# More filler matmuls in the opening of a fused cross-attention and ReGLU kernel

## The chip, the core and the metric

The kernel runs on one core of one Trainium2 chip. The metric is the time of one execution on the device, in microseconds (us). A core has a matrix engine (TensorE, "PE" in the profile, with its weight loads as "PEld"), a vector engine (DVE), a scalar engine (ACT), a general engine (POOL) and a queue engine (SP); each takes its own instructions in order and waits on semaphores for the others. Data comes and goes by DMA.

## The reference

Two stages, the first feeding the second. B = 8 batches, H = 8 heads, S = 512 tokens, Ns = 32 state rows and D = 64.

```python
scores = scale * x @ state^T                 # per batch and head
xread  = softmax(scores) @ state             # 512 rows per batch
sread  = softmax(scale * state @ x^T) @ x    # 32 rows per batch
t = concat([xread, sread]), heads side by side         # 4352 x 512
out = (relu(t @ w_gate) * (t @ w_val)) @ w_out         # 512 -> 1536 -> 512
```

The inputs are float32; the kernel multiplies in bfloat16 and adds in float32.

## The kernel before, in words

For the 512 token rows of a batch, attention output times `w_gate` is never formed in two steps. The kernel multiplies the state by the weights first (`U`, made by `c_unit` for 256 columns of both weights or by `u_unit` for 512 columns of one) and then multiplies the softmax weights by `U` (`gv`). Twelve column blocks `jf` of 128 give the gated product `h_sb`, and the last product with `w_out` (`o_half`) is built from seven half-sized products, for which POOL makes sums and differences (`h_sums`, `h_last`).

The order of the first three and a half batches is written out by hand. A text, `program`, is a list of steps such as `xT.0.1`; a table, `steps`, maps each name to a function, and a loop calls them in turn. A step emits its instructions at the end of the queues of the engines that it uses, so the list fixes the order on each engine, and only semaphores move one engine against another. The steps that matter here, for batch 0:

- `spin.n`: n matmuls of 512 columns on a zeroed tile `warm` (line 572), into a PSUM bank of their own (`warm_ps`) that nobody reads. These are the fillers.
- `stc`, `stT`, `sto`: cast the state of batches 0 and 1, transpose it on PE (line 149), copy it to SBUF (line 156).
- `xh`: cast `x` for two heads; `xT.0.j`: transpose it on PE (lines 182 and 184); `xo.0.j`: copy the transpose out on DVE or ACT (line 188).
- `sc.0.k`: scores on PE (line 199); `ex`: exponential on ACT (line 203); `nr`: sum and reciprocal on DVE (lines 209 and 211); `nx`: scaling on DVE (line 215).
- `aT.0.k`: transpose of the softmax weights on PE (line 231); `ao`: copy out on DVE (line 235).
- `c.k.i`: state times weight columns on PE (line 311), where k = 0 and 1 are the batch and i is the block of 256 columns; `co`: copy out on ACT or DVE (line 331).
- `ga` and `gb`: the first and second half of the product with `U` on PE (line 336); `re` and `mu`: ReLU on ACT (line 363) and product on DVE (line 367).

PE's small results rotate through six PSUM banks, so a step can also wait until the copy of an older result has freed a bank.

The weights come in twelve DMAs of 256 columns each (`w_dma`, line 134), issued by POOL in the order gate, value, gate, value and so on, with batch 1 of `x` after the first four. Block i of `c` needs the i-th gate and value pieces. After batch 3 the rest of the schedule comes from loops with slots.

Of the kernel before, what the change touches and what calls it, by code (L numbers as in the profile page):

```python
# [16 lines left out]
def kernel(  # L17
# [9 lines left out]
    nc = tc.nc  # L27
# [38 lines left out]
    warm = gpool.tile([128, 512], BF16, name="warm", tag="g_sb")  # L66
# [6 lines left out]
    stT = const.tile([128, B, NJ, 64], BF16, name="stT")  # L73
# [4 lines left out]
    xf, xb, xT, e_sn, a_sn, ANS, U, hsb, sr_sb = {}, {}, {}, {}, {}, {}, {}, {}, {}  # L78
    copy = {"act": nc.scalar.copy, "dve": nc.vector.tensor_copy, "pool": nc.gpsimd.tensor_copy}

    def bank(name, o=None):

        if o is None:
            return ps_r.tile([128, 512], FP32, name=name, tag="r")
        return ps_o.tile([128, 512], FP32, name=name, tag=f"o{o}")
# [73 lines left out]
    def x_conv(b, half, eng):  # L159
        if half == 0:  # L160
            xb_alloc(b)
            xb[b] = xb[b].rearrange("p (c h d) -> p c h d", c=NC, h=H)
        hs = slice(HK * half, HK * half + HK)
        copy[eng](out=xb[b][:, :, hs].rearrange("p c h d -> p h c d"), in_=xf[b][:, hs])
# [387 lines left out]
    ws = ((moe_w_gate, wg_sb), (moe_w_val, wv_sb))  # L552
# [15 lines left out]
    warm_ps = bank("warm_ps", "w")  # L568
# [4 lines left out]

    def x_cast(b, i, eng):
        x_conv(b, i, eng)

    steps = {"spin": spin, "stc": state_conv, "stT": state_T, "sto": state_out, "xT": x_T, "xo": x_out,
             "sc": att_sc, "ex": att_exp, "nr": att_sum, "nx": att_scale, "aT": att_T, "ao": att_out,  # L580
             "c": c_unit, "co": c_out, "u": u_unit, "uo": u_out, "ga": lambda b, jf: gv(b, jf, (0,)),
             "gb": lambda b, jf: gv(b, jf, (1,)), "re": relu, "mu": mult, "oh": o_half, "oc": o_c, "oa": o_a, "os": o_s,
             "hs": h_sums, "hl": h_last, "ws": w_sum, "xd": lambda b: x_dma(b, (nc.sync,)), "xg": lambda b: x_dma(b, (nc.gpsimd,)),
             "xh": x0_cast, "xc": x_cast,
             "xt": x_trans_dma, "aD": att_aT_dma, "srp": sr_pre, "srl": sr_low, "srm": sr_mm, "srn": sr_norm}
    program = """
    spin.7 stc.0.2.dve stT.0.2 sto.0.2.1.act sto.0.2.0.dve xh.0.dve xT.0.0 xo.0.0.dve xh.1.act xT.0.1
    xo.0.1.dve xT.0.3 xo.0.3.act sc.0.0 ex.0.0 xT.0.2 nr.0.0 nx.0.0 xo.0.2.act sc.0.1 ex.0.1 spin.1 c.0.0
    c.1.0 spin.1 nr.0.1 nx.0.1 aT.0.0 ao.0.0.dve spin.1 aT.0.1 co.0.0.0.act ga.0.0 co.1.0.0.act co.1.0.1.dve
    co.0.0.1.act ao.0.1.dve xg.3 c.0.1 co.0.1.0.act co.0.1.1.dve c.1.1 co.1.1.0.dve gb.0.0 re.0.0 mu.0.0  # L590
    ga.0.2 gb.0.2 re.0.2 mu.0.2 co.1.1.1.act ga.0.3 gb.0.3 re.0.3 ga.0.1 gb.0.1 xT.1.0 xT.1.1 re.0.1 xT.1.2
    mu.0.3 mu.0.1 xo.1.1.dve xT.1.3 xo.1.3.dve c.0.2 c.1.2 xo.1.0.act xo.1.2.act sc.1.0 sc.1.1 co.0.2.0.act
    ga.0.5 co.0.2.1.dve gb.0.5 c.0.3 co.1.2.0.dve ex.1.0 nr.1.0 co.1.2.1.act re.0.5 nx.1.0 ex.1.1 nr.1.1
    mu.0.5 co.0.3.1.act co.0.3.0.act ga.0.4 aT.1.0 ao.1.0.dve gb.0.4 re.0.4 c.1.3 co.1.3.1.act c.0.4
    co.1.3.0.act ga.0.6 gb.0.6 mu.0.4 co.0.4.1.act ga.0.7 gb.0.7 co.0.4.0.dve re.0.6 re.0.7 mu.0.6 nx.1.1.pool
    aT.1.1 ga.0.9 ao.1.1.act gb.0.9 re.0.9 mu.0.7 ga.0.8 gb.0.8 re.0.8 ga.1.0 ga.1.1 mu.0.9 mu.0.8 gb.1.0
    re.1.0 mu.1.0 gb.1.1 re.1.1 ga.1.6 gb.1.6 ga.1.2 ga.1.3 gb.1.3 re.1.6 re.1.3 gb.1.2 stT.2.4 ga.1.5 mu.1.1
    gb.1.5 ga.1.4 re.1.2 gb.1.4 ga.1.7 gb.1.7 mu.1.6 mu.1.3 hs.0.0 sto.2.4.0.dve oh.0.0 re.1.5 re.1.7 mu.1.2
    mu.1.5 re.1.4 xT.2.0 xT.2.2 mu.1.7 sto.2.4.1.dve xo.2.0.act c.0.5 mu.1.4 co.0.5.0.act xo.2.2.dve xT.2.3
    xT.2.1 co.0.5.1.dve xo.2.1.dve c.1.5 co.1.5.1.dve ga.0.11 co.1.5.0.act gb.0.11 ga.0.10 xo.2.3.dve gb.0.10  # L600
    hs.0.1 re.0.11 mu.0.11 re.0.10 mu.0.10 sc.2.0 ex.2.0 nr.2.0 ga.1.10 gb.1.10 re.1.10 sc.2.1 ex.2.1 ga.1.11
    gb.1.11 u.2.1.0 oh.0.1 nx.2.0 aT.2.0 re.1.11 uo.2.1.0.0.act mu.1.11 uo.2.1.0.1.act mu.1.10 u.2.0.0 c.1.4
    ws.0.pool ao.2.0.act oh.0.2 oh.0.3 co.1.4.0.dve xc.3.0.act ws.1.pool oc.0.1 hs.0.2 ga.1.8 oh.0.4 ga.1.9
    co.1.4.1.act gb.1.8 xc.3.1.pool xt.3 uo.2.0.0.0.act nr.2.1 re.1.8 nx.2.1.pool oa.0.3 ws.2.pool oh.0.6
    uo.2.0.0.1.act ws.3.pool mu.1.8 oh.0.5 hl.0 gb.1.9 aT.2.1 re.1.9 mu.1.9 xd.4 oc.0.5 ga.2.0 ga.2.1
    xc.4.0.pool xc.4.1.pool ao.2.1.act hs.1.0 oh.0.7 gb.2.0 hs.1.2 re.2.0 mu.2.0 ga.2.3 gb.2.3 gb.2.1 xt.4
    re.2.1 re.2.3 hs.1.1 ga.2.2 gb.2.2 oh.0.8 mu.2.1 mu.2.3 re.2.2 u.2.1.1024 uo.2.1.1024.0.act u.2.0.1024
    uo.2.0.1024.1.act oh.0.9 oc.0.9 mu.2.2 u.2.1.512 u.2.0.512 uo.2.0.512.0.act sc.3.0 uo.2.0.1024.0.dve
    uo.2.1.512.1.act oh.0.10 uo.2.1.512.0.dve ga.2.5 oa.0.9 ex.3.0 oh.0.12 oh.0.13 uo.2.1.1024.1.act ga.2.4
    uo.2.0.512.1.act gb.2.4 re.2.4 oh.0.11 oc.0.11 ga.2.7 gb.2.5 oh.1.0 mu.2.4 sc.3.1 ga.2.6 gb.2.6 nr.3.0  # L610
    os.0.11 oa.0.13 srm.0 re.2.5 nx.3.0 mu.2.5 srn.0 ex.3.1 gb.2.7 re.2.6 re.2.7 xd.5 ga.2.8 gb.2.8 re.2.8
    mu.2.7 oh.1.1 mu.2.6 oh.1.2 nr.3.1 mu.2.8 u.3.0.0 uo.3.0.0.0.act u.3.1.0 oh.1.3 uo.3.0.0.1.act u.3.0.512
    uo.3.0.512.0.act nx.3.1 aD.3 uo.3.0.512.1.act oc.1.1 oa.1.3 ga.2.9 gb.2.9 re.2.9 srm.1 stT.4.8
    sto.4.8.1.act oh.1.4 sto.4.8.0.act oh.1.5 ga.2.10 gb.2.10 re.2.10 srn.1 mu.2.9 oc.1.5 ga.2.11 gb.2.11
    re.2.11 oh.1.6 oh.1.7 uo.3.1.0.1.dve mu.2.10 u.3.1.512 u.3.1.1024 hs.2.0 hl.1 u.3.0.1024 uo.3.1.0.0.act
    mu.2.11 oh.1.8 xc.5.0.dve uo.3.1.512.0.act sc.4.0 uo.3.1.1024.1.dve ga.3.0 gb.3.0 uo.3.1.512.1.act hs.2.1
    ga.3.1 gb.3.1 oh.1.9 xc.5.1.pool ga.3.2 gb.3.2 ex.4.0 uo.3.1.1024.0.act hs.2.2 uo.3.0.1024.1.dve re.3.0
    re.3.1 mu.3.1 oc.1.9 oa.1.9 mu.3.0 re.3.2 mu.3.2 ga.3.3 gb.3.3 srm.2 srn.2 re.3.3 mu.3.3 xd.6 oh.1.10
    oh.1.11 nr.4.0 nx.4.0 oc.1.11 xt.5 uo.3.0.1024.0.dve os.1.11
    """  # L620
    for word in program.split():
        name, *args = word.split(".")
# [91 lines left out]
```

## Time and profile before

| what | value |
|---|---|
| time, median of 3 runs | 223.88 us (223.65 to 223.88) |
| the profiled execution's own time | 224.46 us |
| span of the profile, first to last instruction | 222.4 us |
| PE busy | 212.3 us, 95% of the span |
| DVE, ACT, POOL busy | 155.2 us (70%), 127.1 us (57%), 165.4 us (74%) |

The span lies 2.06 us under the profiled execution's own time, which has what comes before the first and after the last instruction. Times in the profile count from the span's start. A row of the timeline gives start, duration, engine, line, operation, result and operands, how many instructions are merged in it, and in brackets the idle time before it with what ended it. A row of several matmuls lasts from the first start to the last end; a matmul's duration includes its way through the array, so neighbours overlap, and the spacing of starts tells the rate.

### The profile page before, as it was taken

The numbers are of one execution on the slowest core, as the hardware profiler recorded it, in microseconds if no ns is written. First come the engines' busy times: TensorE is split into PE (matmuls) and PEld (weight loads), VectorE is DVE, ScalarE is ACT, GpSimd is POOL, SyncE is SP. The second block draws the span as 40 slices with busy tenths as digits, with TensorE's granted clock in tenths as the row PEclk, the third lists the DMA queues.
The fourth block names the chain that finished last, engine by engine and source line by source line (L and its number), as shares of the span: only waits on it lengthen the run. The fifth ranks groups of instructions, "written<-read, shape, count | busy, mean of one in ns | idle before, by whom it ended". The sixth has DMA issues, their size and how long they took to land.

```text
span 222.4 us, 5490 instructions
## 1 busy us (share of the span) xinstructions
PE 212.3 (95%) x2194; PEld 139.0 (63%) x2194; DVE 155.2 (70%) x272; ACT 127.1 (57%) x240; POOL 165.4 (74%) x163
## 2 busy tenths in 40 slices
PE   6699999999999999999999999999999999999991
PEld 1445445475666657656765676567656666888880
DVE  3579877964488969978787878787877485433521
ACT  2558966886766773575557655765566444322330
POOL 7956389899899999399949993995399619924130
PEclk9999999999999999999999999999999999999998
DMA  7999999139196308810399047102310121031015
GB/s 161 174 193 195 196 197 280 42 28 270 39 236 203 83 12 248 216 49 4 82 228 213 0 109 177 50 0 97 95 47 4 47 99 47 1 102 67 25 57 179
DMA packets 42329, 25.32 MB, mean 114 GB/s; under 512 B 18816, under 2 KB 41856, under 8 KB 42304
## 3 DMA queue, kind: packets, MB, share of 16 engines
q1 hardware_dynamic: 28992, 16.65, 28.6%
q0 software_dynamic: 12480, 7.54, 22.4%
q10 hardware_dynamic: 832, 0.79, 1.0%
q8 instruction: 17, 0.28, 0.5%
q14 instruction: 8, 0.07, 0.1%
HBM read 18.35 MB, written 8.91 MB: 123 GB/s over the span
## 4 chain that ended last, share of the span: by engine, by line
PE 82%; POOL 7%; ACT 3%; DVE 2%; DMA 2%; issue 1%; DVEq 0%; POOLq 0%
PE gv_ps L336 33%; PE w_ps L434 16%; PE z_ps L434 12%; PE gv_ps L354 5%; PE up L311 4%; PE sc_ps L199 2%; PE upc L311 2%; DMA st_f<-in_state_dram 2%; POOL s L398 2%; POOL s L397 2%; POOL h_sb L406 2%; POOL h_sb L399 1%; PE zs_ps L434 1%; PE ws_ps L434 1%; DVE h_sb L367 1%
## 5 line engine op out<-in xcount | busy, mean ns | idle before, releaser
L367 DVE TENSOR_TENSOR h_sb<-gv_ps,g_sb 128x512 bf16<-128x512 f32 (+1 forms) x108 | 69.3, 657 | 39.2 <-ACT g_sb L363 30.4
L336 PE MATMUL gv_ps<-ans,U 128*128 128x512 bf16 x384 | 95.7, 380 | 0.3 <-DVE U L331 0.2
L363 ACT ACTIVATE g_sb<-gv_ps 128x512 bf16<-128x512 f32 (+1 forms) x108 | 61.7, 576 | 37.5 <-PE gv_ps L336 27.5
L434 PEld LDWEIGHTS <-h_sb 128*128 128x128 bf16 x516 | 49.5, 98 | 15.8 <-issue 1.7
L336 PEld LDWEIGHTS <-U 128*128 128x128 bf16 x384 | 35.8, 98 | 31.4 <-issue 2.4
L397 POOL TENSOR_TENSOR s<-h_sb 128x512 bf16<-128x512 bf16 x24 | 28.1, 1172 | 18.9 <-DVE h_sb L367 18.9
L406 POOL TENSOR_TENSOR h_sb<-h_sb,s 128x512 bf16<-128x512 bf16 x24 | 27.5, 1172 | 7.1 <-PE z_ps L434 7.1
L398 POOL TENSOR_TENSOR s<-s,h_sb 128x512 bf16<-128x512 bf16 x24 | 28.1, 1169 | 1.9
L444 ACT COPY o_sb<-w_ps 128x512 f32<-128x512 f32 x32 | 18.8, 586 | 18.3 <-PE w_ps L434 18.3
L321 ACT CAST U<-up 128x512 bf16<-128x512 f32 x42 | 22.4, 593 | 11.7 <-PE up L311 11.7
L399 POOL TENSOR_TENSOR h_sb<-h_sb 128x512 bf16<-128x512 bf16 x24 | 28.2, 1174 | 0.0
L434 PE MATMUL w_ps<-wo_sb,h_sb 128*128 128x256 bf16 x192 | 26.2, 273 | 0.0
L434 PEld LDWEIGHTS <-s 128*128 128x128 bf16 x204 | 19.3, 98 | 7.8 <-issue 3.0
L434 PE MATMUL z_ps<-wo_sb,h_sb 128*128 128x256 bf16 x186 | 24.1, 273 | 0.0
L321 DVE CAST U<-up 128x512 bf16<-128x512 f32 x30 | 19.1, 683 | 0.9 <-PE up L311 0.9
L450 DVE TENSOR_TENSOR o_sb<-z_ps,o_sb 128x512 f32<-128x512 f32 (+1 forms) x23 | 15.4, 672 | 4.4 <-PE z_ps L434 2.4
L209 DVE TENSOR_REDUCE cs<-e_sn 128x16 f32<-128x512 bf16 x16 | 10.9, 679 | 5.7 <-ACT e_sn L203 5.7
L434 PE MATMUL w_ps<-t2w,s 128*128 128x256 bf16 x96 | 13.0, 273 | 0.0
L203 ACT ACTIVATE e_sn<-sc_ps 128x512 bf16<-128x512 f32 x16 | 9.6, 600 | 4.8 <-PE sc_ps L199 4.8
L434 PE MATMUL z_ps<-t,s 128*128 128x256 bf16 x90 | 12.0, 273 | 0.0
L434 PE MATMUL w_ps<-t,h_sb 128*128 128x256 bf16 x96 | 12.0, 273 | 0.0
L215 DVE TENSOR_TENSOR a_sn<-e_sn,rc 128x512 bf16<-128x512 bf16 x14 | 10.8, 768 | 0.4
(89 smaller groups left out, 225.7 us busy)
## 6 DMA issues: line engine op xcount, KB each, us to landing
out_dram<-o_sb SPq DMA_DIRECT2D x30, 256.0 KB, 2.3
xf<-in_x_dram SPq DMA_DIRECT2D x4, 1024.0 KB, 6.9
wg_sb<-in_moe_w_gate_dram POOLq DMA_DIRECT2D x6, 256.0 KB, 10.1
wv_sb<-in_moe_w_val_dram POOLq DMA_DIRECT2D x6, 256.0 KB, 10.3
wo_sb<-in_moe_w_out_dram POOLq DMA_DIRECT2D x2, 768.0 KB, 15.4
xf<-in_x_dram POOLq DMA_DIRECT2D x1, 1024.0 KB, 19.2
xb<-in_x_dram POOLq DMA_DIRECT2D x3, 256.0 KB, 8.2
xb<-in_x_dram POOLq DMA_DIRECT2D x1, 512.0 KB, 11.4
```

The source lines that it names most:

```text
L311: nc.tensor.matmul(dst[kc][q:q + 32], stT[r:r + 64, b, j, 32 * sl:32 * sl + 32], wsb[r:r + 64, j, lo:lo + n], start=True, stop=True)
L321: copy[eng](out=U[b][:, w, kc, lo:lo + 512], in_=held["u", b, w, lo][kc])
L336: nc.tensor.matmul(ps[w], U[b][:, w, kc, f0:f0 + 128], ANS[b][:, kc].rearrange("p c t -> p (c t)"), start=(kc == 0), stop=(kc == NK - 1))
L363: nc.scalar.activation(out=g_sb[:, 0:n], in_=ps[0][:, 0:n], func=AF.Relu)
L367: nc.vector.tensor_tensor(out=dst, in0=ps[1][:, 0:n], in1=held["g", b, jf][:, 0:n], op=ALU.mult)
L397: tt(out=s_block(b, 1, i), in0=a21, in1=a22, op=ALU.add)
L398: tt(out=s_block(b, 2, i), in0=s_block(b, 1, i), in1=a11, op=ALU.subtract)
L399: tt(out=a21, in0=a11, in1=a21, op=ALU.subtract)
L406: {"dve": nc.vector, "pool": nc.gpsimd}[eng].tensor_tensor(out=a12, in0=a12, in1=s_block(b, 2, i), op=ALU.subtract)
L434: nc.tensor.matmul(ps[:, HM * c + lo:HM * c + hi], a[:, i, 128 * c:128 * c + 128], w[:, i, lo:hi], start=(i == 0 and (p in ("p1", "p2", "p ...
L444: nc.scalar.copy(out=o_sb, in_=held["acc", b, "w", 0])
L450: nc.vector.tensor_tensor(out=o_sb[:, cols], in0=banks[c if isinstance(c, int) else 0][:, cols], in1=o_sb[:, cols], op=ALU.add)
```

## The change

The list of steps keeps its order. What changes is the fillers between the steps. A new step `sq.n` gives n short fillers of 128 columns.

```diff
+    def spin_short(n):
+        for i in range(n):
+            nc.tensor.matmul(warm_ps[:, 0:128], warm[:, 0:128], warm[:, 0:128], start=True, stop=True)
...
     program = """
-    spin.7 stc.0.2.dve stT.0.2 sto.0.2.1.act sto.0.2.0.dve xh.0.dve xT.0.0 xo.0.0.dve xh.1.act xT.0.1
-    xo.0.1.dve xT.0.3 xo.0.3.act sc.0.0 ex.0.0 xT.0.2 nr.0.0 nx.0.0 xo.0.2.act sc.0.1 ex.0.1 spin.1 c.0.0
-    c.1.0 spin.1 nr.0.1 nx.0.1 aT.0.0 ao.0.0.dve spin.1 aT.0.1 co.0.0.0.act ga.0.0 co.1.0.0.act co.1.0.1.dve
+    spin.9 stc.0.2.dve stT.0.2 spin.1 spin.1 sto.0.2.1.act sq.2 sto.0.2.0.dve sq.2 sq.2 xh.0.dve spin.1 spin.1
+    xT.0.0 xo.0.0.dve sq.1 xh.1.act xT.0.1 xo.0.1.dve xT.0.3 xo.0.3.act sc.0.0 ex.0.0 xT.0.2 nr.0.0 spin.1
+    nx.0.0 xo.0.2.act sq.2 sq.2 sq.2 sc.0.1 ex.0.1 sq.2 spin.1 spin.1 sq.1 c.0.0 c.1.0 nr.0.1 nx.0.1 aT.0.0
+    ao.0.0.dve aT.0.1 co.0.0.0.act ga.0.0 co.1.0.0.act co.1.0.1.dve
```

Counted on PE, in order:

| place | fillers before | fillers after |
|---|---|---|
| ahead of `stT` | 7 x 512 | 9 x 512 |
| between `stT` and `xT.0.0` | none | 2 x 512, 6 x 128, 2 x 512 |
| between `xT.0.0` and `xT.0.1` | none | 1 x 128 |
| between `xT.0.2` and `sc.0.1` | none | 1 x 512, 6 x 128 |
| between `sc.0.1` and `c.0.0` | 1 x 512 | 2 x 128, 2 x 512, 1 x 128 |
| between `c.1.0` and `aT.0.0` | 1 x 512 | none |
| between `aT.0.0` and `aT.0.1` | 1 x 512 | none |
| columns in all | 5120 | 10240 |

All other instructions, on every engine, are the same and in the same order.

More of the change, by code (lines that the diff above doesn't have):

```diff
@@ L572, in spin @@
             nc.tensor.matmul(warm_ps, warm[:, 0:128], warm, start=True, stop=True)
+    def spin_short(n):
+        for i in range(n):
+            nc.tensor.matmul(warm_ps[:, 0:128], warm[:, 0:128], warm[:, 0:128], start=True, stop=True)
     def x_cast(b, i, eng):
         x_conv(b, i, eng)
-    steps = {"spin": spin, "stc": state_conv, "stT": state_T, "sto": state_out, "xT": x_T, "xo": x_out,
+    steps = {"spin": spin, "sq": spin_short, "stc": state_conv, "stT": state_T, "sto": state_out, "xT": x_T, "xo": x_out,
              "sc": att_sc, "ex": att_exp, "nr": att_sum, "nx": att_scale, "aT": att_T, "ao": att_out,
@@ L586 @@
     program = """
-    spin.7 stc.0.2.dve stT.0.2 sto.0.2.1.act sto.0.2.0.dve xh.0.dve xT.0.0 xo.0.0.dve xh.1.act xT.0.1
-    xo.0.1.dve xT.0.3 xo.0.3.act sc.0.0 ex.0.0 xT.0.2 nr.0.0 nx.0.0 xo.0.2.act sc.0.1 ex.0.1 spin.1 c.0.0
-    c.1.0 spin.1 nr.0.1 nx.0.1 aT.0.0 ao.0.0.dve spin.1 aT.0.1 co.0.0.0.act ga.0.0 co.1.0.0.act co.1.0.1.dve
-    co.0.0.1.act ao.0.1.dve xg.3 c.0.1 co.0.1.0.act co.0.1.1.dve c.1.1 co.1.1.0.dve gb.0.0 re.0.0 mu.0.0
-    ga.0.2 gb.0.2 re.0.2 mu.0.2 co.1.1.1.act ga.0.3 gb.0.3 re.0.3 ga.0.1 gb.0.1 xT.1.0 xT.1.1 re.0.1 xT.1.2
@@ L592 @@
[L592 to L616, printed above, removed]
@@ L617 @@
-    ga.3.1 gb.3.1 oh.1.9 xc.5.1.pool ga.3.2 gb.3.2 ex.4.0 uo.3.1.1024.0.act hs.2.2 uo.3.0.1024.1.dve re.3.0
-    re.3.1 mu.3.1 oc.1.9 oa.1.9 mu.3.0 re.3.2 mu.3.2 ga.3.3 gb.3.3 srm.2 srn.2 re.3.3 mu.3.3 xd.6 oh.1.10
-    oh.1.11 nr.4.0 nx.4.0 oc.1.11 xt.5 uo.3.0.1024.0.dve os.1.11
+    spin.9 stc.0.2.dve stT.0.2 spin.1 spin.1 sto.0.2.1.act sq.2 sto.0.2.0.dve sq.2 sq.2 xh.0.dve spin.1 spin.1
+    xT.0.0 xo.0.0.dve sq.1 xh.1.act xT.0.1 xo.0.1.dve xT.0.3 xo.0.3.act sc.0.0 ex.0.0 xT.0.2 nr.0.0 spin.1
@@ new lines @@
+    nx.0.0 xo.0.2.act sq.2 sq.2 sq.2 sc.0.1 ex.0.1 sq.2 spin.1 spin.1 sq.1 c.0.0 c.1.0 nr.0.1 nx.0.1 aT.0.0
+    ao.0.0.dve aT.0.1 co.0.0.0.act ga.0.0 co.1.0.0.act co.1.0.1.dve co.0.0.1.act ao.0.1.dve xg.3 c.0.1
+    co.0.1.0.act co.0.1.1.dve c.1.1 co.1.1.0.dve gb.0.0 re.0.0 mu.0.0 ga.0.2 gb.0.2 re.0.2 mu.0.2 co.1.1.1.act
+    ga.0.3 gb.0.3 re.0.3 ga.0.1 gb.0.1 xT.1.0 xT.1.1 re.0.1 xT.1.2 mu.0.3 mu.0.1 xo.1.1.dve xT.1.3 xo.1.3.dve
+    c.0.2 c.1.2 xo.1.0.act xo.1.2.act sc.1.0 sc.1.1 co.0.2.0.act ga.0.5 co.0.2.1.dve gb.0.5 c.0.3 co.1.2.0.dve
@@ new lines @@
+    ex.1.0 nr.1.0 co.1.2.1.act re.0.5 nx.1.0 ex.1.1 nr.1.1 mu.0.5 co.0.3.1.act co.0.3.0.act ga.0.4 aT.1.0
+    ao.1.0.dve gb.0.4 re.0.4 c.1.3 co.1.3.1.act c.0.4 co.1.3.0.act ga.0.6 gb.0.6 mu.0.4 co.0.4.1.act ga.0.7
+    gb.0.7 co.0.4.0.dve re.0.6 re.0.7 mu.0.6 nx.1.1.pool aT.1.1 ga.0.9 ao.1.1.act gb.0.9 re.0.9 mu.0.7 ga.0.8
+    gb.0.8 re.0.8 ga.1.0 ga.1.1 mu.0.9 mu.0.8 gb.1.0 re.1.0 mu.1.0 gb.1.1 re.1.1 ga.1.6 gb.1.6 ga.1.2 ga.1.3
+    gb.1.3 re.1.6 re.1.3 gb.1.2 stT.2.4 ga.1.5 mu.1.1 gb.1.5 ga.1.4 re.1.2 gb.1.4 ga.1.7 gb.1.7 mu.1.6 mu.1.3
@@ new lines @@
+    hs.0.0 sto.2.4.0.dve oh.0.0 re.1.5 re.1.7 mu.1.2 mu.1.5 re.1.4 xT.2.0 xT.2.2 mu.1.7 sto.2.4.1.dve
+    xo.2.0.act c.0.5 mu.1.4 co.0.5.0.act xo.2.2.dve xT.2.3 xT.2.1 co.0.5.1.dve xo.2.1.dve c.1.5 co.1.5.1.dve
+    ga.0.11 co.1.5.0.act gb.0.11 ga.0.10 xo.2.3.dve gb.0.10 hs.0.1 re.0.11 mu.0.11 re.0.10 mu.0.10 sc.2.0
+    ex.2.0 nr.2.0 ga.1.10 gb.1.10 re.1.10 sc.2.1 ex.2.1 ga.1.11 gb.1.11 u.2.1.0 oh.0.1 nx.2.0 aT.2.0 re.1.11
+    uo.2.1.0.0.act mu.1.11 uo.2.1.0.1.act mu.1.10 u.2.0.0 c.1.4 ws.0.pool ao.2.0.act oh.0.2 oh.0.3
@@ new lines @@
+    co.1.4.0.dve xc.3.0.act ws.1.pool oc.0.1 hs.0.2 ga.1.8 oh.0.4 ga.1.9 co.1.4.1.act gb.1.8 xc.3.1.pool xt.3
+    uo.2.0.0.0.act nr.2.1 re.1.8 nx.2.1.pool oa.0.3 ws.2.pool oh.0.6 uo.2.0.0.1.act ws.3.pool mu.1.8 oh.0.5
+    hl.0 gb.1.9 aT.2.1 re.1.9 mu.1.9 xd.4 oc.0.5 ga.2.0 ga.2.1 xc.4.0.pool xc.4.1.pool ao.2.1.act hs.1.0
+    oh.0.7 gb.2.0 hs.1.2 re.2.0 mu.2.0 ga.2.3 gb.2.3 gb.2.1 xt.4 re.2.1 re.2.3 hs.1.1 ga.2.2 gb.2.2 oh.0.8
+    mu.2.1 mu.2.3 re.2.2 u.2.1.1024 uo.2.1.1024.0.act u.2.0.1024 uo.2.0.1024.1.act oh.0.9 oc.0.9 mu.2.2
@@ new lines @@
+    u.2.1.512 u.2.0.512 uo.2.0.512.0.act sc.3.0 uo.2.0.1024.0.dve uo.2.1.512.1.act oh.0.10 uo.2.1.512.0.dve
+    ga.2.5 oa.0.9 ex.3.0 oh.0.12 oh.0.13 uo.2.1.1024.1.act ga.2.4 uo.2.0.512.1.act gb.2.4 re.2.4 oh.0.11
+    oc.0.11 ga.2.7 gb.2.5 oh.1.0 mu.2.4 sc.3.1 ga.2.6 gb.2.6 nr.3.0 os.0.11 oa.0.13 srm.0 re.2.5 nx.3.0 mu.2.5
+    srn.0 ex.3.1 gb.2.7 re.2.6 re.2.7 xd.5 ga.2.8 gb.2.8 re.2.8 mu.2.7 oh.1.1 mu.2.6 oh.1.2 nr.3.1 mu.2.8
+    u.3.0.0 uo.3.0.0.0.act u.3.1.0 oh.1.3 uo.3.0.0.1.act u.3.0.512 uo.3.0.512.0.act nx.3.1 aD.3
@@ new lines @@
+    uo.3.0.512.1.act oc.1.1 oa.1.3 ga.2.9 gb.2.9 re.2.9 srm.1 stT.4.8 sto.4.8.1.act oh.1.4 sto.4.8.0.act
+    oh.1.5 ga.2.10 gb.2.10 re.2.10 srn.1 mu.2.9 oc.1.5 ga.2.11 gb.2.11 re.2.11 oh.1.6 oh.1.7 uo.3.1.0.1.dve
+    mu.2.10 u.3.1.512 u.3.1.1024 hs.2.0 hl.1 u.3.0.1024 uo.3.1.0.0.act mu.2.11 oh.1.8 xc.5.0.dve
+    uo.3.1.512.0.act sc.4.0 uo.3.1.1024.1.dve ga.3.0 gb.3.0 uo.3.1.512.1.act hs.2.1 ga.3.1 gb.3.1 oh.1.9
+    xc.5.1.pool ga.3.2 gb.3.2 ex.4.0 uo.3.1.1024.0.act hs.2.2 uo.3.0.1024.1.dve re.3.0 re.3.1 mu.3.1 oc.1.9
@@ L620 @@
+    oa.1.9 mu.3.0 re.3.2 mu.3.2 ga.3.3 gb.3.3 srm.2 srn.2 re.3.3 mu.3.3 xd.6 oh.1.10 oh.1.11 nr.4.0 nx.4.0
+    oc.1.11 xt.5 uo.3.0.1024.0.dve os.1.11
     """
```

## The prediction

> **What bounds the kernel now.** I read the page first, then PE's timeline of the first 26 us, then ACT's and DVE's for the same stretch, then the landing of the weight DMAs.
>
> ```profile
> PE   6699999999999999999999999999999999999991
> ...
> PEclk9999999999999999999999999999999999999998
> ...
> PE 82%; POOL 7%; ACT 3%; DVE 2%; DMA 2%; issue 1%; DVEq 0%; POOLq 0%
> ```
>
> PE is busy nine tenths or more in every slice but the first two and the last, and 82% of the chain that ended last is PE. So time won on PE early should stay won to the end, unless something that does not move with PE (a DMA) becomes late. The clock row shows full speed from the start. The matmuls say otherwise:
>
> ```profile
> 1.19 3.17 PE L572 MATMUL warm_ps<-warm 128*128 128x512 bf16 x7 [1.19 <-DVE warm L529]
> 4.98 0.39 PE L149 MATMUL stT_ps<-id,st_b 128*128 128x128 bf16 x2 [0.63 <-DVE st_b L143]
> 6.83 1.03 PE L184 MATMUL xT_ps<-id,xb 128*128 128x128 bf16 x8 [1.45 <-DVE xb L541]
> 8.36 0.61 PE L199 MATMUL sc_ps<-stT,xT 128*128 128x64 bf16 x8
> 10.22 0.61 PE L199 MATMUL sc_ps<-stT,xT 128*128 128x64 bf16 x8 [0.69 <-ACT xT L188]
> 10.64 0.61 PE L572 MATMUL warm_ps<-warm 128*128 128x512 bf16 x1
> 11.18 0.41 PE L311 MATMUL upc<-wg_sb,stT 64*32 64x256 bf16 x8
> 13.42 0.63 PE L231 MATMUL aT_ps<-id,a_sn 128*128 128x128 bf16 x4
> 13.85 1.06 PE L336 MATMUL gv_ps<-ans,U 128*128 128x512 bf16 x2
> 14.84 0.42 PE L311 MATMUL upc<-wg_sb,stT 64*32 64x256 bf16 x8
> 15.03 0.44 PE L311 MATMUL upc<-wv_sb,stT 64*32 64x256 bf16 x8
> 15.83 3.19 PE L336 MATMUL gv_ps<-ans,U 128*128 128x512 bf16 x14
> 20.88 0.64 PE L199 MATMUL sc_ps<-stT,xT 128*128 128x64 bf16 x16
> 22.32 0.30 PE L311 MATMUL upc<-wg_sb,stT 64*32 64x256 bf16 x8
> 22.43 0.29 PE L311 MATMUL upc<-wv_sb,stT 64*32 64x256 bf16 x8
> 23.71 0.40 PE L231 MATMUL aT_ps<-id,a_sn 128*128 128x128 bf16 x4 [0.39 <-DVE a_sn L215]
> ```
>
> One 512-column matmul lasts 0.61 us at 10.64, so seven in 3.17 us are spaced by (3.17 - 0.61) / 6 = 0.43 us. From 15.83 fourteen take 3.19 us; with a last one of 0.38 us (the mean of line 336 in the page is 380 ns) the spacing is (3.19 - 0.38) / 13 = 0.216 us, half. So PE runs at half speed until about 15.8 us and at full speed from there, although the clock row shows nothing; I take it that the record of the clock begins only with that switch. Half speed does exist in the record, at the other end:
>
> ```profile
> 10.22:15.83 5.61, 5.61 (x86) 1.00 1.43 191
> 220.70:222.40 1.70, 0.00 (x0) 0.50 0.02 7
> ```
>
> These are rows of the windows view for PE (window, length, busy, clock, DMA share, GB/s). After the last matmul the granted clock is 0.50. And the switch at 15.8 came after 5.61 us in which PE was busy throughout, while the 3.17 us of the first fillers, followed by 0.63 us of idling, did not bring it. So unbroken work opens the gate, after more than 3.2 and at most 5.6 us.
>
> **The change part by part.** *Fillers ahead of the first transposes.* Nine fillers from 1.19 issue for 9 x 0.427 = 3.84 us, to about 5.02, against the 4.98 at which `stT` becomes ready: 0.03 us late at most. Two more of 512 columns go on to about 6.1 at half speed, six of 128 (a quarter of 0.427 us each) to 6.7, two of 512 to 7.6. PE is then busy from 1.19 without a break. By the bounds above the gate opens between 1.19 + 3.2 = 4.4 and 1.19 + 5.6 = 6.8 us; I take the middle, 5.6. From 5.6 on, the rest of the fillers costs half: about 0.25 us for the second long one, 6 x 0.054 us, 2 x 0.216 us, so they end at 6.6, ahead of the 6.83 at which `xT.0.0` has its cast. They are hidden by the wait for DVE's cast of `x` (1.45 us of idle PE before the change). If the gate opens only at 6.8, they end at about 7.2 and the cover is exceeded by 0.35 us.
>
> The Trainium skill, "TensorE: Matmul & The Clock Gate", Part 1, says that the gate looks at free-running windows of about 3.4 us and opens after one busy window. Counted back from 15.85 by such steps, one window is 2.19 to 5.61, which the fillers now fill; by that rule the opening is at 5.6 in this run and the sum stays the same, but the phase of the windows may differ from run to run, which the runs shown cannot tell.
>
> *What the full clock is worth up to the first big products.* The engines that PE feeds:
>
> ```profile
> 9.00 0.60 ACT L203 ACTIVATE e_sn<-sc_ps 128x512 bf16<-128x512 f32 x1
> 9.58 0.59 ACT L188 COPY xT<-xT_ps 128x512 bf16<-128x512 bf16 x1
> 10.86 0.60 ACT L203 ACTIVATE e_sn<-sc_ps 128x512 bf16<-128x512 f32 x1 [0.70 <-PE sc_ps L199]
> 11.85 1.56 ACT L331 CAST U<-upc 128x512 bf16<-128x512 f32 x3 [0.39 <-PE upc L311]
> 7.47 0.85 DVE L188 COPY xT<-xT_ps 128x512 bf16<-128x512 bf16 x2 [0.70 <-PE xT_ps L184]
> 10.64 0.69 DVE L215 TENSOR_TENSOR a_sn<-e_sn,rc 128x512 bf16<-128x512 bf16 x1
> 11.49 0.69 DVE L209 TENSOR_REDUCE cs<-e_sn 128x16 f32<-128x512 bf16 x1 [0.16 <-ACT e_sn L203]
> 12.50 0.69 DVE L215 TENSOR_TENSOR a_sn<-e_sn,rc 128x512 bf16<-128x512 bf16 x1
> 13.24 0.42 DVE L235 COPY ans<-aT_ps 128x512 bf16<-128x512 bf16 x1
> 13.58 0.68 DVE L331 CAST U<-upc 128x512 bf16<-128x512 f32 x1
> 14.18 0.41 DVE L235 COPY ans<-aT_ps 128x512 bf16<-128x512 bf16 x1
> ```
>
> I follow the chain with these durations and shorter matmuls.
> - Four transposes take 0.63 us slow (13.42) and 0.40 fast (23.71). `xT.0.0` at 6.85 is done at 7.25, DVE's two copies start at 7.27 in place of 7.47: 0.20 earlier.
> - Scores: 0.61 us slow; fast, sixteen take 0.64, so eight end after about 0.40. They start 0.20 earlier and end 0.41 earlier: `ex.0.0` at 8.60 in place of 9.00, the copy behind it at 9.18 in place of 9.58, `sc.0.1` at 9.82 in place of 10.22. The fillers between `xT.0.2` and `sc.0.1` are 0.22 + 6 x 0.054 = 0.54 us in a hole that was 0.69 us and stays about as long: hidden.
> - `sc.0.1` wins 0.21 again, so `ex.0.1` is at 10.25 in place of 10.86. DVE still has `nx.0.0` until 10.24 + 0.69 = 10.93, so `nr.0.1` starts at 10.95 in place of 11.49: 0.54 earlier. That carries down DVE's queue: second `nx` at 11.96, `ao.0.0` at 12.70, `co.1.0.1` at 13.04, `ao.0.1` at 13.64, done at 14.05.
> - PE: `sc.0.1` has issued by 10.05; fillers of 1408 columns, 0.60 us, to 10.65; `c.0.0` and `c.1.0` there in place of 11.18, at about 0.12 us for each eight matmuls (22.32 and 22.43) in place of 0.20. ACT's copies start at about 11.1 in place of 11.85 and stay ahead of DVE. Then PE waits for `nx.0.1` and does `aT.0.1` at 12.7.
> - `ga.0.0` waits for DVE's `ao.0.0`, done 13.12: at 13.2 in place of 13.85. Two matmuls of 0.216 us, then `c.0.1` at 13.75 in place of 14.84. `c.1.1` and `gb.0.0` need `ao.0.1` of 14.05, so `c.1.1` runs at 14.1 and `gb.0.0` at 14.4 in place of 15.83: **1.4 us earlier**.
>
> The two fillers that leave behind `c.1.0` and `aT.0.0` each took an issue slot of 0.43 us; what their going saves is in these starts.
>
> *What is late next.* The weights come at the pace of the DMA queues, whatever PE does. Issue rows of POOL, and from the DMA view the time from issue to landing of the two value pieces that they belong to:
>
> ```profile
> 8.53 0.77 POOL L134 DMA_DIRECT2D wv_sb<-in_moe_w_val_dram  x1
> wv_sb<-in_moe_w_val_dram POOLq DMA_DIRECT2D x1, 256.0 KB, 10.0
> 10.10 0.75 POOL L134 DMA_DIRECT2D wv_sb<-in_moe_w_val_dram  x1
> wv_sb<-in_moe_w_val_dram POOLq DMA_DIRECT2D x1, 256.0 KB, 11.1
> 20.09 0.36 PE L311 MATMUL upc<-wv_sb,stT 64*32 64x256 bf16 x8
> ```
>
> The third value piece lands at 18.5 and is used at 20.09; with 1.4 us taken off, at 18.7, just behind it. The fourth lands at 21.2 and is used at 22.43 (above); with 1.4 us off it would be wanted at 21.03. So about 0.2 us of the gain goes there and **1.2 us** is left. ACT and DVE are nearly full at this place, but their work hangs on PE and moves with it:
>
> ```profile
> 20.00:25.00 5.00, 4.46 (x94) 1.99 (x93) 4.89 (x11) 4.68 (x10) 2.85 (x4) 1.00 1.45 198
> ```
>
> Here the columns after the length are PE, PEld, DVE (4.89 of 5 us), ACT (4.68) and POOL. For their small shifts I take off another 0.1, so the sum is **-1.1 us**: 224.46 becomes 223.4 for a profiled execution (span 221.3), and 223.88 becomes 222.8 for the median of the runs. That median lies 0.58 us under the profiled execution's own time, and I take the same distance after the change. The end of the gain is between 0.9 (gate at 6.8) and 1.4 (no loss at the landings).
>
> **The rivals.** *The gate opens late.* If it opens only when the fillers at half speed have ended at 7.6, `xT.0.0` waits 0.75 us for them. The chain above, started 0.75 later and with the same savings behind it, brings `gb.0.0` about 0.6 us earlier than before in place of 1.4, and no landing limits it: -0.5 us, 223.4. For it: nothing shows which 3.2 to 5.6 us count. Against: the fillers begin at 1.19 and leave no hole. The free-running windows that the skill's page describes would make such a case in some runs.
>
> *The gate closes again (slower).* The two fillers behind `c.1.0` go, so PE idles from about 11.4 to 12.7, where `aT.0.1` waits for DVE. If such thin work lets the gate fall back to half before 12.7, PE must work anew for up to 5.6 us, to 18.3 or, with the small holes there, 19.3. Then `gb.0.0` comes at about 14.95, ten of the fourteen products run at 0.43 us until 19.3 and the last four at 0.216, to 20.1, where they ended issuing at 15.83 + 14 x 0.216 = 18.85: +1.3 us, 225.2. It decides the sign if the clock is still low past about 16.5. Against it: in the profile the half clock is granted only after PE's last matmul, and the hole is 1.3 us. The same page (Part 1, "HAM oscillation") puts the idle time that closes the gate at more than about 3.4 us; by that rule the price is nothing.
>
> *The gain is eaten.* DVE at 4.89 of 5 us, the landings, or a transfer that meets another later on give back all but 0.2: 223.7. For it: 18% of the chain is not PE. Against: the weights are the only transfers with a fixed pace, and behind them everything waits for PE.
>
> *The gate does not open early at all.* All fillers run slow, and `gb.0.0` comes about 0.5 us late: 224.4. The fillers are the same zero matmuls that stood in the unbroken stretch, so I hold this for unlikely.
>
> **How the numbers follow.** Forecast (-0.9 to -1.4): 0.56. Late gate: 0.14. Gain eaten: 0.14. Gate closes: 0.10. No early gate: 0.06. About 0.2% (0.45 us) is what a measurement of this kernel can tell from no change. The forecast and two thirds of the late gate lie beyond it: faster 0.65. The rest of the late gate, and the eaten gain within 0.45 us: same 0.17. The gate that closes, no early gate, and an eaten gain that goes over into a loss: slower 0.18. The range runs from 222.2 (the full 1.4 us and 0.3 for knock-on gains) to 224.4 (no early gate); the closing gate is left out.
>
> **What would show it.** Right: in the changed profile 512-column fillers at 0.216 us spacing by 6.8 us, `xT.0.0` within 0.1 us of 6.83, `gb.0.0` near 14.4, no half-speed matmul after 7, the value piece of `c.0.3` waited for near 21.2, and the span 1.1 us shorter. Wrong: `xT.0.0` at 7.5, products of 0.43 us spacing after 12.7, a `gb.0.0` that is early while the products with `w_out` later on are not.

## The result and the profile after

The changed kernel takes 222.75 us in the median of 5 runs (222.48 to 223.28), the kernel before 223.76 us (223.31 to 223.88, 5 runs beside them). The ratio is 0.9961, 95% interval 0.9944 to 0.9979: 0.2 to 0.6% faster. A second set of 12 runs (222.59 us) gives 0.9957 (0.9936 to 0.9977).

The page of the changed kernel, the lines that answer to those shown of before:

```profile
span 220.8 us, 5534 instructions
...
PE   7989999999999999999999999999999999999991
...
PEclk9999999999999999999999999999999999999997
...
PE 82%; POOL 7%; DVE 4%; ACT 3%; issue 1%; DVEq 0%; POOLq 0%
```

The span is 1.6 us shorter, and 1.4 of it is won in the first slices. PE's timeline of the changed kernel:

```profile
1.19 4.02 PE L572 MATMUL warm_ps<-warm 128*128 128x512 bf16 x9 [1.19 <-DVE warm L529]
5.00 0.42 PE L149 MATMUL stT_ps<-id,st_b 128*128 128x128 bf16 x2
5.22 1.06 PE L572 MATMUL warm_ps<-warm 128*128 128x512 bf16 x2
6.07 0.85 PE L578 MATMUL warm_ps<-warm 128*128 128x128 bf16 x6
6.71 0.65 PE L572 MATMUL warm_ps<-warm 128*128 128x512 bf16 x2
7.20 0.39 PE L184 MATMUL xT_ps<-id,xb 128*128 128x128 bf16 x4
...
9.98 0.41 PE L199 MATMUL sc_ps<-stT,xT 128*128 128x64 bf16 x8 [0.16 <-ACT xT L188]
...
10.92 0.30 PE L311 MATMUL upc<-wg_sb,stT 64*32 64x256 bf16 x8
...
12.85 0.40 PE L231 MATMUL aT_ps<-id,a_sn 128*128 128x128 bf16 x4 [0.97 <-DVE a_sn L215]
13.18 0.59 PE L336 MATMUL gv_ps<-ans,U 128*128 128x512 bf16 x2
13.70 0.30 PE L311 MATMUL upc<-wg_sb,stT 64*32 64x256 bf16 x8
...
14.44 3.19 PE L336 MATMUL gv_ps<-ans,U 128*128 128x512 bf16 x14
...
21.04 0.29 PE L311 MATMUL upc<-wv_sb,stT 64*32 64x256 bf16 x8
```

Four transposes last 0.39 us from 7.20 on, where they took 0.63 before, and the eight scores at 9.98 last 0.41 in place of 0.61: PE is at full speed from about 7. The trace's record of the granted clock begins at 6.82. `gb.0.0`, the first of the fourteen products, is at 14.44 in place of 15.83. The same instructions of the two profiles stay 1.39 us apart to 24 us, 1.40 at 70 us and 1.55 to 1.58 from 86 us to the last product. DVE, which sets the pace between the scores and the products, in the changed kernel:

```profile
11.10 0.68 DVE L209 TENSOR_REDUCE cs<-e_sn 128x16 f32<-128x512 bf16 x1
...
12.10 0.69 DVE L215 TENSOR_TENSOR a_sn<-e_sn,rc 128x512 bf16<-128x512 bf16 x1
12.71 0.41 DVE L235 COPY ans<-aT_ps 128x512 bf16<-128x512 bf16 x1
13.04 0.68 DVE L331 CAST U<-upc 128x512 bf16<-128x512 f32 x1
13.64 0.41 DVE L235 COPY ans<-aT_ps 128x512 bf16<-128x512 bf16 x1
```

### The profile page after: what moved, and what is told of

It is laid out like the page before. It is cut to its first block, busy times and chain, and to the rows that moved or that the text cites. A ratio compares the mean times of both kernels' runs of the same rounds, so it can differ in the third digit from the quotient of the medians.

```text
span 220.8 us, 5534 instructions
## 1 busy us (share of the span) xinstructions
PE 212.3 (96%) x2216; PEld 139.5 (63%) x2216; DVE 155.0 (70%) x272; ACT 126.8 (57%) x240; POOL 165.1 (75%) x163
## 4 chain that ended last, share of the span: by engine, by line
PE 82%; POOL 7%; DVE 4%; ACT 3%; issue 1%; DVEq 0%; POOLq 0%
PE gv_ps L336 33%; PE w_ps L434 17%; PE z_ps L434 12%; PE gv_ps L354 5%; PE up L311 4%; PE warm_ps L572 2%; POOL s L398 2%; POOL s L397 2%; POOL h_sb L399 2%; POOL h_sb L406 2%; PE zs_ps L434 1%; PE sc_ps L199 1%; DVE h_sb L367 1%; PE ws_ps L434 1%; POOL es_f L275 1%
## 5 line engine op out<-in xcount | busy, mean ns | idle before, releaser
L399 POOL TENSOR_TENSOR h_sb<-h_sb 128x512 bf16<-128x512 bf16 x24 | 27.7, 1154 | 0.0
L215 DVE TENSOR_TENSOR a_sn<-e_sn,rc 128x512 bf16<-128x512 bf16 x14 | 11.8, 846 | 0.4
```

Of the source, the lines that this page charges most:

```text
L215: (nc.gpsimd if eng == "pool" else nc.vector).tensor_tensor(out=a_sn[b][:, kc].rearrange("p c (h n) -> p (c h) n", n=Ns), in0=e_v, in1=hel ...
L399: tt(out=a21, in0=a11, in1=a21, op=ALU.subtract)
```

## The experiments

Four experiments take the change apart; then the changed kernel is repeated beside three variants of it; then the kernel before is profiled three times more. All but the last three have 11 or 12 runs of their own and 33 to 35 of the kernel before on the same chip; each leaves one profile. A row of the windows view gives window, length, busy time of PE, clock, DMA share and GB/s. Where an expectation speaks of the busy share of a 3.4 us stretch, a matmul counts for its duration less 0.17 us of way through the array, and overlaps count once. The windows view counts whole durations, so its busy times are larger. A profile can lack the record of a matmul; where that changes a reading, the text says so. The granted clock in a result is the mean over a run's span. One window of 3.41 us at half speed lowers it by 0.0077 (half of 3.41 in 221); the half speed after the last matmul lowers it by up to about 0.006. Time before the first opening is in no record, so it does not lower it. Between two changes of the granted clock the profiles show 3.41 us or whole multiples of it; each such stretch of 3.41 us is called a window here, and where the windows lie in a run its phase. The gate opens when full speed is granted and closes when it goes back to half. The edits below show the steps concerned, without the line breaks of the list.

**The middle fillers alone.** The edit, on the kernel before:

```diff
-    xT.0.2 nr.0.0 nx.0.0 xo.0.2.act sc.0.1 ex.0.1 spin.1 c.0.0 c.1.0 spin.1 nr.0.1 nx.0.1 aT.0.0 ao.0.0.dve spin.1 aT.0.1
+    xT.0.2 nr.0.0 nx.0.0 xo.0.2.act sc.0.1 ex.0.1 c.0.0 c.1.0 nr.0.1 nx.0.1 aT.0.0 ao.0.0.dve aT.0.1
```

> The kernel before, without its three fillers of 512 columns around `c.0.0`, `c.1.0` and `aT.0.0`; nothing is added ahead. Theory (the gain is the clock gate that opens earlier): three issue slots of 0.43 us go, but `aT.0.1` still waits for DVE, so `gb.0.0` wins 0.2 us at most; PE now idles before `aT.0.1`, its unbroken work begins only at about 13.2, the gate opens between 16.5 and 18.9 in place of 15.8, and products run at 0.43 us spacing until then: 0.2 to 1.4 us slower than before, about 0.6 (224.4). Rival (the gain is the slots that the change takes out of the middle): 0.4 to 0.9 us faster than before.

224.75 us, ratio 1.0058 (1.0036 to 1.0080): slower, as the theory said and against the rival. The windows view of PE in the profiled run shows one way in which it comes about, divided where the clock record changes:

```profile
0.49:3.90 3.41, 2.71 (x7) 1.00 0.51 155
3.90:7.32 3.42, 1.55 (x21) 1.00 1.41 212
7.32:10.73 3.41, 2.62 (x56) 0.50 1.29 163
10.73:14.14 3.41, 2.51 (x42) 0.50 1.43 189
14.14:17.56 3.42, 3.09 (x38) 0.50 1.45 197
17.56:20.97 3.41, 3.37 (x68) 1.00 1.45 196
```

The record begins at 3.90 here (the 1.00 ahead of it is only the lack of a record). The seven fillers did open the gate; the thin stretch up to 7.32 closed it; it took a dense stretch, 14.14 to 17.56, to open it again, within the 16.5 to 18.9 that were expected for a first opening. This run took 223.81 us and is one of three with a clock of 0.976 or 0.977. The nine others have 0.997 or more and up to 225.84 us; by that clock no window closed in them, and how late their gate first opened no profile shows. Taking slots out of the middle does not help by itself: in the profiled run it thins the work and keeps the clock low for longer.

**The early fillers alone.** On the changed kernel:

```diff
-    xT.0.2 nr.0.0 spin.1 nx.0.0 xo.0.2.act sq.2 sq.2 sq.2 sc.0.1 ex.0.1 sq.2 spin.1 spin.1 sq.1 c.0.0 c.1.0 nr.0.1 nx.0.1 aT.0.0 ao.0.0.dve aT.0.1
+    xT.0.2 nr.0.0 nx.0.0 xo.0.2.act sc.0.1 ex.0.1 spin.1 c.0.0 c.1.0 spin.1 nr.0.1 nx.0.1 aT.0.0 ao.0.0.dve spin.1 aT.0.1
```

> The fillers up to `xT.0.1` as after the change, everything behind as before: the three fillers of 512 columns around `c.0.0` and `aT.0.0` back, none between `xT.0.2` and `sc.0.1`. Theory: the gate opens by 7 us as after the change; at full clock the three fillers cost 0.22 us each and lie in holes (the one ahead of `c.0.0` replaces 0.60 us of others), so the time is that of the changed kernel within 0.2 us, 222.7, `gb.0.0` near 14.4. Rival (the slots in the middle): most of the gain is gone, 223.4 or more. Rival (the later fillers are needed to keep the gate open): half-speed products behind 12, 223.8 or more.

223.11 us, ratio 0.9976 (0.9956 to 0.9995). It is faster than before, with a clock of 0.994 or more in every run, so the three old fillers are enough to keep the gate open. The time lies between what the theory (222.7 within 0.2) and the first rival (223.4 or more) gave: by the medians the early fillers alone bring 0.24% where the whole change brings 0.39 to 0.43%, but the intervals overlap, so their share is not settled. The products do not come later than in the changed kernel: the trace records thirteen of the fourteen, from 14.34, and the first, which lacks its record, belongs near 14.1. Compared with the profile of before, the lead is 1.71 us at 17 us; then 0.27 us of it goes where PE waits for the fourth value piece, and 0.6 us between 43 and 47 us, where a transpose waits that follows without a wait in the changed kernel's profile:

```profile
21.06 0.30 PE L311 MATMUL upc<-wv_sb,stT 64*32 64x256 bf16 x8 [0.16 <-DMA wv_sb<-in_moe_w_val_dram]
...
43.59 0.40 PE L231 MATMUL aT_ps<-id,a_sn 128*128 128x128 bf16 x4 [0.40 <-ACT U L321]
```

Whether that has to do with the later fillers is not shown.

**Without the bridge.** On the changed kernel:

```diff
-    spin.9 stc.0.2.dve stT.0.2 spin.1 spin.1 sto.0.2.1.act sq.2 sto.0.2.0.dve sq.2 sq.2 xh.0.dve spin.1 spin.1 xT.0.0 xo.0.0.dve sq.1 xh.1.act
+    spin.9 stc.0.2.dve stT.0.2 sto.0.2.1.act sto.0.2.0.dve xh.0.dve xT.0.0 xo.0.0.dve xh.1.act
```

> The changed kernel without its eleven fillers between `stT` and `xT.0.1`: PE works unbroken only from 1.19 to about 5.2 (4.0 us), then idles until 6.83. Theory: that is within the 3.2 to 5.6 us that the gate needs by the first trace, so the run tells where in it the need lies. If 4.0 us is enough, the time is that of the changed kernel (222.7); if not, the later fillers run at half speed (1.0 us in a hole of 0.7 ahead of `sc.0.1`, 1.2 us ahead of `c.0.0`), the gate opens around 12 to 14 and the time lies between the two kernels, about 223.4. A spread of runs wider than 0.8 us speaks for windows with a free phase. Rival (the fillers matter as delays, not through the clock): within 0.1 us of the changed kernel whatever the spacing of the matmuls.

222.75 us, ratio 0.9971 (0.9952 to 0.9991): not told from the changed kernel, but in its own way. The windows of its profile:

```profile
1.11:4.52 3.41, 3.33 (x8) 1.00 0.73 203
4.52:7.93 3.41, 1.82 (x21) 1.00 1.44 194
7.93:11.35 3.42, 3.17 (x33) 0.50 1.33 173
11.35:14.76 3.41, 2.86 (x76) 1.00 1.43 192
```

Four us of work in one window opened the gate, the idle stretch ahead of `xT.0.0` closed it for one window, and the later fillers opened it again at 11.35, in time for the products. Nine of 12 runs have the clock of about one closed window (0.989 to 0.992). The spread is 222.38 to 224.34. The rival's outcome (the same time) came, but with half-speed matmuls in between, so this experiment alone does not part the two. It also shows that a closed window costs little where it ends ahead of the products: the nine runs have a median of 222.75 us, the three without one took 222.58, 222.67 and 224.34 us.

**Nothing behind the first transposes.** On the changed kernel:

```diff
-    xT.0.2 nr.0.0 spin.1 nx.0.0 xo.0.2.act sq.2 sq.2 sq.2 sc.0.1 ex.0.1 sq.2 spin.1 spin.1 sq.1 c.0.0
+    xT.0.2 nr.0.0 nx.0.0 xo.0.2.act sc.0.1 ex.0.1 c.0.0
```

> The changed kernel without any filler behind `xT.0.1`: the early ones open the gate, then PE is left as thin as the steps make it from 8 to 13 us. Theory (only work as good as none closes the gate): full speed throughout, time of the changed kernel within 0.3 us, 222.7. Rival (thin work closes it): products at 0.43 us spacing behind 13, `gb.0.0` late, 223.8 to 225.2.

223.50 us, ratio 1.000 (0.9972 to 1.0028): the whole gain is gone. The rival is right here. Windows, and from PE's timeline the row of the products:

```profile
4.91:8.32 3.41, 3.07 (x40) 1.00 1.44 193
8.32:11.73 3.41, 1.73 (x53) 1.00 1.43 190
11.73:15.15 3.42, 2.44 (x39) 0.50 1.45 197
15.15:18.56 3.41, 3.41 (x8) 0.50 1.46 197
18.56:21.97 3.41, 3.37 (x81) 1.00 1.45 196
```

```profile
15.15 4.66 PE L336 MATMUL gv_ps<-ans,U 128*128 128x512 bf16 x13 [0.34 <-issue]
```

(Thirteen of fourteen: the first, near 14.73, lacks its record.) Opened at 4.91, the gate closes at 11.73 after a window that is half busy, although the longest hole of PE up to there is 0.82 us, and stays closed until 18.56. Until then the products go at 0.43 us spacing, eight in 3.41 us; this run took 224.81 us. The 12 runs sort by their clock:

| clock | closed windows | runs | time, median and range |
|---|---|---|---|
| 0.995 to 0.996 | none | 3 | 222.48 (222.28 to 222.81) |
| 0.989 to 0.991 | one | 7 | 223.64 (223.16 to 225.28) |
| 0.985 | two | 2 | 224.81 and 225.07 |

All of these runs have the same steps in the same order, and the three in which no window closed are all faster than the nine others, by 1.2 us in the median, and as fast as the changed kernel. This is the strongest evidence here that the gate, and not the placing of the fillers as delays, carries the gain; one run with a single closed window, at 225.28 us, is slower than the clock explains. It also gives the later fillers their use: in the changed kernel they keep the gate open.

**The changed kernel again.**

> The changed kernel once more, for comparison on this chip. Theory (the gate judges windows of 3.4 us whose phase differs from run to run; opens on a window of 0.8 busy or more, closes on one of 0.3 or less): it opens between 3.9 and 7.4 in every run and never closes, because no 3.4 us stretch behind it is less than 0.47 busy; granted clock 0.994 or more in every run, 0.3 to 0.5% faster than before, 222.4 to 222.9. Rival (the first traces were a lucky phase): some runs with a clock of 0.99 or less, and times of 223.5 or more in these.

222.59 us, ratio 0.9957 (0.9936 to 0.9977). Clock 0.994 to 1.000 in all 12 runs, and the opening in the profile is at 5.20. So it does not close, as expected. But two runs took 223.36 and 224.02 at clocks of 1.000 and 0.994: the rival's slow times without the rival's clock, and the clock does not explain these two.

The profile shows a second thing that varies. Here the gate opened early, and the products lead those of before by 1.76 us at 17 us, more than the 1.39 us of the first profile. Then PE waits for the third, fourth and fifth value pieces in turn:

```profile
18.93 0.30 PE L311 MATMUL upc<-wv_sb,stT 64*32 64x256 bf16 x8 [0.35 <-DMA wv_sb<-in_moe_w_val_dram]
21.58 0.30 PE L311 MATMUL upc<-wv_sb,stT 64*32 64x256 bf16 x8 [0.40 <-DMA wv_sb<-in_moe_w_val_dram]
24.28 0.30 PE L311 MATMUL upc<-wv_sb,stT 64*32 64x256 bf16 x8 [0.29 <-DMA wv_sb<-in_moe_w_val_dram]
```

At 26.5 us the lead is 0.95 us: 0.8 us went back. The profile of the variant with fewer fillers behind (below) shows the same three waits, that of the early fillers alone one. Whether late weights also made the two slow runs, no profile shows.

**A shorter bridge.** On the changed kernel:

```diff
-    sq.2 sq.2 xh.0.dve spin.1 spin.1 xT.0.0
+    sq.2 sq.2 xh.0.dve xT.0.0
```

> The changed kernel without the two fillers of 512 columns right ahead of `xT.0.0`. Theory: at half speed the bridge then ends at 6.75 in place of 7.2 to 7.6, so `xT.0.0` is not held up where the gate opens late; up to 0.3 us faster than the changed kernel in these runs, 0.1 in the median (222.6), if the window that judges is still 0.8 busy. Rival (the gate needs the whole bridge): runs where it opens late or closes, 223.2 or more in the median.

222.83 us, ratio 0.9967 (0.9942 to 0.9993). Its fastest run is 221.89 and its profile has a span of 220.0 us, but the median is no better than that of the changed kernel. Inconclusive.

**The hole filled.** On the changed kernel:

```diff
-    c.0.0 c.1.0 nr.0.1 nx.0.1 aT.0.0 ao.0.0.dve aT.0.1
+    c.0.0 c.1.0 nr.0.1 nx.0.1 aT.0.0 ao.0.0.dve spin.1 spin.1 spin.1 aT.0.1
```

> The changed kernel with three fillers of 512 columns more in the hole ahead of `aT.0.1` (0.65 us in a hole of about 1 us). Theory: nothing closes the gate there in the changed kernel, so nothing is won or lost: within 0.1 us of it. Rival (in some phases the thin stretch closes the gate): 0.2 us or more faster in the median, and a narrower spread.

222.98 us, ratio 0.9972 (0.9954 to 0.9990): nothing won. The median is 0.39 us above that of the changed kernel where the theory allowed 0.1, but the intervals overlap. The range is narrower (222.46 to 223.50 against 222.02 to 224.02), but its clocks are those of the changed kernel except for one run at 0.993, so filling the hole changes nothing about the gate.

**Fewer fillers behind.** On the changed kernel:

```diff
-    sc.0.1 ex.0.1 sq.2 spin.1 spin.1 sq.1 c.0.0
+    sc.0.1 ex.0.1 c.0.0
```

> The changed kernel without the fillers between `sc.0.1` and `c.0.0` (1408 columns), those ahead of `sc.0.1` kept. Theory: the thinnest 3.4 us stretch is then about 0.35 busy, between the 0.31 that closed the gate and the 0.44 that did not: if it stays open in every run, 222.7 as the changed kernel; if it closes in some, these have a clock of 0.985 to 0.992 and take 0.5 to 2 us longer. Rival (those fillers only delay `c.0.0` by 0.6 us): 0.2 us or more faster in every run.

223.20 us, ratio 0.9979 (0.9960 to 0.9997). The rival is refuted: no faster than the changed kernel. Four of 12 runs have the clock of one closed window (0.990 to 0.992) and a median of 223.37; the other eight have 222.80, but three of these took 223.31 to 223.40, so the two groups overlap. In the profiled run the thinnest window left the gate open:

```profile
8.71:12.12 3.41, 1.99 (x56) 1.00 1.40 184
```

One filler at about 8.8 us lacks its record, so the busy time is 2.15 us rather than 1.99. At that it stayed open; at 1.82 (without the bridge) and 1.73 (nothing behind) it closed. This variant sits close to the edge, and it fits that the phase decides.

**The kernel before, three profiles.**

> The kernel before, unchanged, one look. Theory (windows with a phase that differs): in about half of the looks a window that ends between 3.9 and 4.9 is 0.75 busy or more, so its seven fillers open the gate early, the idle stretch up to 6.83 closes it one window later, near 7.3 to 8.3, and it opens again near 14 to 17.5; granted clock 0.98. In the others it opens first between 12.5 and 17.5 as in the first trace, clock 0.994 or more. Rival (the phase is fixed at the kernel's start): the opening at 15.8 again.

> The kernel before, a second look, with the same expectations: an opening at another time than in the first look speaks for a free phase, one at the same time for the rival.

> The kernel before, a third look, with the same expectations: an opening at another time than in the first two looks speaks for a free phase, one at the same time for the rival.

222.93, 222.82 and 224.11 us. The first two opened at 4.09 and 4.51, closed at 7.50 and 7.92, and opened again at 14.33 and 14.75; the third opened first at 15.96. So the phase is free. Windows and the products of the first, then the products of the third (this row runs to 17 us only):

```profile
0.68:4.09 3.41, 2.90 (x7) 1.00 0.56 172
4.09:7.50 3.41, 1.28 (x19) 1.00 1.42 202
7.50:10.92 3.42, 2.65 (x43) 0.50 1.31 166
10.92:14.33 3.41, 3.41 (x44) 0.50 1.44 192
```

```profile
14.95 3.29 PE L336 MATMUL gv_ps<-ans,U 128*128 128x512 bf16 x14
```

```profile
15.83 1.52 PE L336 MATMUL gv_ps<-ans,U 128*128 128x512 bf16 x6
```

The 68 runs of the kernel before beside the experiments fall in groups by clock: 31 at 0.979 to 0.983 with a median of 223.44 us, 11 at 0.996 to 0.998 with 224.30, 26 at the other values with about 223.3. The profile from which the prediction was made has 0.996 and 224.46 us: it belongs to the slowest group. That 0.979 to 0.983 means an early opening with two closed windows is seen in two of the three profiles above (0.980 and 0.981); for the other runs it is read from the clock.

## Why the prediction was right

The forecast was 222.8 us, the result 222.75. The mechanism held: the fillers open the gate early, and the first products come 1.4 us sooner. That the figures meet within 0.05 us is luck; some terms were off and cancelled.

- *The gate opens early and PE then works at full speed:* right. With the changed kernel's early fillers it opened at 6.82, 5.20, 5.94, 4.91, 5.30 and 7.07 in six profiles, against a forecast of 4.4 to 6.8 with 5.6 as the middle: two lie at or beyond the late end. In what decides it the step was wrong: not 3.2 to 5.6 us of unbroken work, but the share of one window. The 3.2 us of seven fillers are enough when they fall into one window (0.80, 0.85 and 0.88 of it opened the gate) and not when they are split (0.62 and 0.65 did not).
- *The fillers are hidden:* not quite in the profiled run. They ended at 7.2 and held up `xT.0.0` to 7.20, 0.37 us late, the upper end that was given. Full speed and the hole ahead of `sc.0.1` swallowed it: 9.98 where 9.82 was forecast, and PE's idle time there fell from 0.69 to 0.16 us. In the repeated changed kernel, where the gate opened at 5.20, they were hidden: `xT.0.0` ran at 6.82 after 0.25 us of idle PE.
- *The chain:* right, with two small errors that cancel. Forecast and measured: `nx.0.1` 11.96 and 12.10, `ao.0.0` 12.70 and 12.71, `co.1.0.1` 13.04 and 13.04, `ao.0.1` 13.64 and 13.64, `gb.0.0` 14.4 and 14.44. The second `nx` was 0.14 us late, with `xT.0.0`. In the profile of before `ao.0.0` starts 0.74 us after it, just as the slow `aT.0.0` ends (12.57 and 0.63 us); the forecast kept that distance, but in the changed kernel `aT.0.0` is long done and the distance is 0.61.
- *0.2 us go back at the fourth value piece, 0.1 on DVE and ACT:* not in the first profile. The piece landed earlier in this run, and its use came 1.39 us earlier with the rest. POOL's issue row, and from the DMA view the time to landing:

```profile
10.03 0.80 POOL L134 DMA_DIRECT2D wv_sb<-in_moe_w_val_dram  x1
```

```profile
wv_sb<-in_moe_w_val_dram POOLq DMA_DIRECT2D x1, 256.0 KB, 10.6
```

 It is there at 20.6 and is used at 21.04. Nothing was given back, and the span lost 1.6 us where 1.1 was forecast. The wait itself was rightly foreseen: in the repeated changed kernel, where the products come earlier still, the same piece took 11.5 us from its issue at 10.00, PE waited for it and for two others, and 0.8 us of the lead went. So the size of this term differs from run to run, from nothing to 0.8 us in the profiles here.
- *The median moves as the profiled execution does:* wrong, and this made up for the step before. The profiled execution went from 224.46 to 222.73, by 1.73 us, the median by 1.0. The profile of before was of an unlucky phase; in a more frequent one (31 of the 68 runs by their clock, and the first two of the three profiles), the old fillers open the gate for a window and the products start at 14.95 or 15.10, not 15.83. So the products of the changed kernel's first profile gain 1.4 us against one phase and 0.5 to 0.7 against the other. The end of a profile adds its own differences: from the last matmul to the end of the span it is 4.35 us in the first of the three profiles and 4.94 in the changed kernel's. The comparison of phases comes from single profiles and groups by clock; the size of each group's gain was not measured by itself.
- *The rival of the closing gate:* it did not happen to the changed kernel, but it is real and was priced near the mark: 225.2 forecast; 224.81 and 225.07 in the runs without later fillers in which the gate stayed closed for two windows. The reason given against it was wrong: a hole of 1.3 us or less is no protection. What protects the changed kernel, as far as the windows tell, is that they stay above the edge:

```profile
3.41:6.82 3.41, 3.41 (x16) 1.00 1.36 241
6.82:10.24 3.42, 3.16 (x52) 1.00 1.37 176
10.24:13.65 3.41, 2.44 (x53) 1.00 1.42 187
```

 The Trainium skill, "TensorE: Matmul & The Clock Gate", Part 1, "HAM oscillation", gives a gap of over about 3.4 us as what closes the gate; the runs here differ, a window of 3.41 us that still has 1.28 to 1.82 us of busy time in the view closes it. Its free-running window of about 3.4 us agrees: the closed stretches measure 3.42, 6.83 and 10.24 us.
- *The gate opens late:* not seen as a case of its own; it is the upper end of the same spread of phases (7.07 in one profile).
- *The gain is eaten:* seen in part, at the landings that the prediction named: 0.8 us of 1.76 in the repeated changed kernel, but not all but 0.2 us of it.

## What to carry to other kernels

Fillers are worth their place when they do two things: bring PE's share of one 3.4 us window to about 0.8 as early as possible, and keep each later window over the edge at which the gate closes; the second half is easily forgotten, and here its lack cost the whole gain of the median. Judge them in the holes they use, since at full speed a filler is half as long as the profile of the slow part suggests. Work that comes earlier can also meet weights that have not landed, and then part of the gain goes back. And where the clock's phase is free, one profile is one draw: take several before measuring a change of half a per cent against it.

## What the hardware showed that was not expected

The clock record of these traces begins with the first opening; until then the clock row reads full speed while matmuls run at half (0.43 us spacing). With the way through the array taken off, the gate opened on windows with a busy share of 0.80 or more and not on 0.72 or less (0.76 in one window, with a matmul that lacks its record counted). It closed on 0.31 or less and stayed open on 0.44 or more, and in one window on 0.34 as recorded, 0.40 with the filler that lacks its record. The windows view as it stands does not part the openings: 2.71 of 3.41 us opened it without the middle fillers, 2.73 did not in the first profile of before. The phase of the windows differs from run to run of the same kernel. No stall marks the closing: in the profiled run without later fillers PE was never idle for more than 0.82 us before it.
